# A new order and new engines for the pieces of a hand-ordered attention and mixture kernel

## The chip, the cores and the metric

The kernel runs on one core of a Trainium2 chip. The metric is the device time of one execution, in microseconds, from three timed runs; a profile of one execution goes with them. The engines of the core are named as in the profile: PE (TensorE), DVE (VectorE), ACT (ScalarE), POOL (GpSimd) and SP (SyncE, which issues all transfers here).

## What is computed

Three stages follow each other; the second takes the first's output as 1152 tokens of 512 features, the third the second's.

```python
# 1: attention, q k v of [2, 8, 576, 64]; four neighbours are averaged for a dense part, 7 neighbours seen by a local one
out_d = sm_attn(q_d, k_d, v_d)                       # on means of four
out_up = np.repeat(out_d, 4, axis=2)
mask = np.abs(pos[:, None] - pos[None, :]) < 4
x = out_up + softmax(where(mask, scale * q @ k.T, -1e9)) @ v
# 2: a rational activation; x [1152, 512], w_in [512, 2048], w_out [2048, 512] (float64)
h = x @ w_in
P = a[0] + a[1] * h + a[2] * h**2 + a[3] * h**3
Q = 1.0 + abs(b[0]) * abs(h) + abs(b[1]) * h**2
x = (P / (Q + 1e-06)) @ w_out
# 3: 8 experts, each token to the best one; w1 [8, 512, 1024], w2 [8, 1024, 512]; at most `capacity` tokens each
e = argmax(x @ w_gate); out = gate * (relu(x @ w1[e]) @ w2[e]), or 0 for a token that is dropped
```

## The kernel before

All work is cut into some 1,380 **pieces**, each a Python closure with a key. `plan_unit` makes those of the attention: a unit `u0` to `u7` is one batch and two heads, with loads (`lq`, `lk`, `lv`), transposes, local scores and their exponentials (`s`, `m`, `e`, `z`), the norm of the local softmax (`n0`, `n1`), the dense part (`ds` to `dp`; `dn` is its norm), the means of four queries, keys and values (`mq`, `mk`, `mv`) and the combination (`co`). `plan_w_in` and `plan_w_out` turn the float64 bits of one block of weights into float32 (`c1`, `c2`, `c3`, on DVE) and split each block into a high and a low part (`h` a cast, `o` a subtraction), since a product is made of three products of parts. `plan_moe1` is one chunk of 288 tokens (`m0` to `m3`) and a pair of the 16 row blocks of `w_in` (`_0` to `_7`): two groups of matmuls (`h0`, `h1`), then the rational function on a [128, 576] tile: `a` is |h|, `u`, `v1` and `v2` the cubic, `q1` and `q2` the denominator, `r1` and `r2` its reciprocal by a logarithm and an exponential, `f1` and `f2` a Newton step, `f3` the product. The first chunk also goes through `w_out` (`gh`, `go` split the result, `y` are the products) and one expert (`w1_`, `w2_`, `f1_`, `f2_`); the other chunks only need the gate's logits (`l`) and the routing (`rt`). A last count (`bd`) decides a branch that isn't taken here.

One table, `ORDER`, sets the order in which all pieces are emitted, and so the order of each engine's queue: every engine runs its instructions in that order, and waits at the first whose inputs are not there. A key may carry an engine (`m1_0_q1:G`): A, V or G for ACT, DVE or POOL. Buffers (44 of the common kind `G`, 5 for loads, 4 single and 2 double PSUM banks) go to the next taker in the order of release, so the table also sets who waits for whose buffer.

```python
def emit(self):                                   # class Plan
    for key, *_ in self.order:
        fn, needs, take, give = self.work[key]
        for t in take:
            self.held[t, key] = self.free[t].pop(0)
        if fn:
            fn()
        for x in give: ...
def q1():                                         # in plan_moe1
    if plan.engine.get(n + "q1") == "A":
        A.activation(out=d["r"], in_=d["z"], func=ACTF.Identity, scale=b1, bias=b0)
    else:
        vg(n + "q1").tensor_scalar(out=d["r"], in0=d["z"], scalar1=b1, scalar2=b0, ...)
```

`vg(key)` is DVE where the table says V, else POOL. The lines of the profile that matter: 383, 388 and 392 are the three conversions `c1`, `c2`, `c3`; 411 the low part of a `w_in` block, 893 that of a `w_out` or expert block; 473 and 476 to 478 the means of queries and keys, 494 and 495 those of values on POOL; 534 and 559 the norms; 726 and 728 `q1` on ACT and POOL; 731 `q2`; 734 and 737 `v1` and `v2`; 746, 749 and 753 `f1`, `f2` and `f3`. `v1` and `v2` read one of their inputs from PSUM; `f1`, `f2`, `f3` and the conversions read SBUF alone.

Of the kernel before, what the change touches and what calls it, by code (L numbers as in the profile page):

```python
# [22 lines left out]
ORDER = """
cz1 ci cm1:V cm2 ck2 warm22 warm9 u1_lq warm38 ck3 ck4 warm37 warm17 warm13 warm42 ck1 warm44 u1_tq u1_lk u1_tk cj:A u0_lq u0_lk u1_lw1
u1_cq:A wi0l u1_lwe u0_tq u1_ck:A cm3 u1_s0 u1_lw0 u1_lv cz0 u1_mq:G u1_mk:V u0_cq:A u0_mq:G u1_m0 wi7l u0_lw1 u1_ds u1_dm u0_tk u0_ck:V
u1_e0 u1_s1 u1_m1 u0_lv u2_lq warm8 u0_s1 u1_z0 u1_de u0_mk:G wi0c1 u1_e1 u0_s0 u1_dz u0_m1 u1_n0:G u1_lt0 wi0c2 u0_e1 u1_z1 u1_dn:G u0_m0
u1_lc0:V u0_ds u1_lt1 wi0c3 u1_lc1:V u0_e0 u1_n1:G u0_lwe u1_lt2 u0_dm u1_mv:G u1_dt0 u0_z0 u0_z1 u2_lk u1_dt1 u1_lc2:A u1_dc0:A u1_dc1:V
u1_lp2 u1_lp1 u0_mv:G u0_n0:V u0_n1:V u0_de wi0h:A u1_dp u1_dx:A u0_dz wi7c1 u1_lp0 u1_co0 u1_co2 u1_co1 u1_j2 u1_j1 u0_lt0 wi7c2 u2_tq
u2_tk wi2l u0_dn:G u0_dt0 u0_lt2 u0_lw0 u0_lc0:A wi0o:G u2_cq:A wi7c3 u2_ck:A wi1l u0_dt1 u3_lq u0_lc2:A u0_dc0:A wi2c1 wi2c2 u0_dc1:A
x0_1h:A u2_s1 u2_mq:G zs u0_lt1 u0_lc1:A u2_s0 u2_m1 u3_lk u0_dp u0_lp0 wi2c3 u2_e1 wi1c1 u2_m0 u0_dx:A wi1c2 u0_lp2 u0_lp1 u2_mk:G u0_co0  # L30
u2_z1 wi7h:V u0_co2 u2_e0 u2_ds u0_j1 cab wi3l u3_tq u2_n1:G u2_z0 u2_n0:G u2_dm u0_co1 wi2h:A u3_tk u2_lt2 u2_lt0 wi1c3 u3_cq:A u3_ck:A
u3_s1 x0_1o:G u2_lc2:V u3_mk:V u2_de u3_m1 u2_lc0:A u2_lt1 cb u3_s0 ccap u2_dz u2_lv wi2o:V u3_mq:G u3_m0 u2_dn:G wi3c1 u3_ds u2_lc1:A
u3_lwe u2_lwe u2_mv:G u2_lw1 u2_lw0 u3_dm u2_dt0 u3_e1 u4_lq u3_lv u4_lk u2_dt1 u2_dc1:V wi3c2 wi5l u3_e0 u3_z1 u2_lp2 wi3c3 ccf u3_z0
u3_n1:G u2_dc0:A u3_de u3_dz u3_lw0 u3_lw1 u3_mv:G u2_dp u2_dx:A u2_lp0 u2_co0 wi3h:A wi1h:A u2_lp1 u3_dn:V u3_lt2 u2_j0 u1_j0 u2_j1 u0_j2
wi7o:G u4_tq u4_tk u3_lc2:A u3_n0:V u2_co1 u2_co2 x0_0h:V u5_lq wi4l u4_cq:A u4_ck:A u4_mk:G u4_mq:G x0_0o:G u3_dt0 u3_lt0 u3_dt1 u3_dc0:V
u3_lt1 u3_lc1:A u3_dc1:A u4_s0 wi1o:V wi3o:V wi5c1 u3_dp u3_lc0:A x0_2h:A u3_lp0 u4_m0 wi5c2 u3_lp1 u3_dx:A u3_co0 wi5c3 u3_co1 u4_e0
u4_s1 x0_3h:A u3_lp2 x0_3o:G u4_m1 u4_ds x0_2o:V u3_co2 wi4c1 u4_z0 u4_dm wi5h:A u3_j1 u2_j2 u5_tq m0_0_h0 u4_e1 wi5o:G u4_n0:G u5_cq:A
wi4c2 u5_lk u4_de cna u5_tk wi4c3 u5_ck:A wi4h:A u4_lt0 wi14l wi6l wi14c1 u4_lt1 u4_dz u4_z1 wi14c2 u4_lc1:A m0_0_h1 u5_s0 u4_lc0:A m0_0_a
m0_0_u:A wi12l wi10l u5_s1 u5_lw0 u5_mq:G u5_lwe u4_lv u0_st wi6c1 u4_dn:G u4_dt0 wi14c3 wi6c2 u5_mk:G m0_0_q1:A wi11l u0_j3 u3_j0 u0_j0
u3_st u4_dc0:A u5_m0 wi12c1 wi6c3 wi6h:A u5_e0 wi10c1 u3_j2 u3_j3 m0_0_v1 u5_m1 u4_n1:G wi4o:G m0_0_q2:G u4_lw0 u4_lwe wi10c2 m0_0_v2  # L40
u4_lw1 m0_0_j u5_z0 wi12c2 wi10c3 wi8l u5_lv u5_e1 u5_ds u4_dt1 u4_mv:G u5_n0:G wi6o:G u4_dc1:A m0_1_h0 m0_1_h1 u5_z1 u5_dm m0_1_a
m0_1_u:A m0_2_h0 u4_lt2 m0_2_h1 wi9l wi12c3 u4_dp m0_0_r1 wi10h:A u5_de m0_1_v1 m0_2_u:A wi11c1 u4_dx:A m0_1_v2 u5_dz m0_1_j u4_lp0 u4_lp1
u5_n1:G wi14h:A u4_lc2:A m0_0_r2 m0_1_q1:G wi11c2 m0_2_v1 u5_lt2 wi11c3 u4_co0 m0_3_h0 m0_0_f1 u5_dn:G m0_1_q2:G u5_lw1 u4_co1 u6_lq
m0_2_a u5_lc2:A wi11h:A u5_lt0 u4_lp2 m0_2_q1:A u5_dt0 u5_dt1 u5_dc1:A m0_1_r1 wi9c1 u5_lc0:A m0_2_v2 m0_0_f2 m0_3_h1 u6_lk u4_j1 m0_2_j
u5_mv:G u6_tq u5_lt1 m0_2_q2:G wi11o:G wi8c1 u5_dc0:A u5_dp wi9c2 m0_3_u:A u6_cq:A wi8c2 u5_lc1:A u5_dx:A wi9c3 u6_mq:G u4_co2 m0_3_v1
wi9h:A u5_lp0 u5_co0 wi13l cwg u6_tk u7_lq wi8c3 u6_ck:A u5_lp1 u5_lp2 u5_co2 wi12h:A m0_3_a wi8h:A m0_1_r2 m0_2_r1 u6_s1 u6_mk:G u7_lk
m0_0_f3 u6_s0 wo1l u1_st u6_lw0 u6_j0 m0_3_v2 m0_3_j u1_j3 wi15l u5_j1 u7_tq u7_cq:A wi8o:G u6_ds wi9o:G u6_lv u6_m1 u6_m0 wi13c1 wi10o:G
u7_tk u7_lw1 zs8 m0_4_h0 m0_4_h1 u6_e1 m0_0_gh:A m0_1_f1 u6_dm u2_st wo2l zs2 wo1c1 m0_1_f2 u6_z1 u7_ck:A wi13c2 u5_co1 u6_e0 u7_s1 u7_s0
# [319 lines left out]

# [886 lines left out]
```

## Time and profile before

| | |
|---|---|
| time, median of 3 runs | 340.23 us (338.97 to 341.45) |
| profiled execution, span from first to last instruction | 340.3 us |
| DVE busy | 311.7 us, 92% |
| PE busy | 278.6 us, 82% |
| POOL busy | 238.3 us, 70% |
| ACT busy | 195.5 us, 57% |
| TensorE clock granted, mean | 0.894 of full |

The profiled execution's span is the median of the timed runs to 0.1 us, so nothing that could be told apart lies around it. Busy time is from the recorded start to the recorded end of each instruction, with overlaps counted once: an engine that has begun an instruction and is kept from running it counts as busy. An instruction of DVE starts some 0.07 us before the one ahead of it has ended, so durations add up to more than the time that passes.

### The profile page before, as it was taken

To read this page: it belongs to the slowest core of one execution; us is meant where nothing else is said; L and a number is where in the kernel's file an instruction comes from. 1 tells how busy PE (TensorE), PEld (TensorE's weight loads), DVE (VectorE), ACT (ScalarE), POOL (GpSimd) and SP (SyncE) were. 2 spreads that over 40 slices of the span, in tenths; PEclk is the share of its full clock that TensorE was granted. 3 is DMA by queue.
4 is the path that set the end of the run, shared out by engine and by line. 5 is a ranking of instruction groups with operands and counts; after the bars stand their busy time and mean duration, and the time that the engine had idled before them with its cause. 6 is when DMAs were issued, how large, how long until landed. Compare 5 with 4: busy or idle time off the path is not lost.

```text
span 340.3 us, 6602 instructions
## 1 busy us (share of the span) xinstructions
PE 278.6 (82%) x2366; PEld 250.9 (74%) x2366; DVE 311.7 (92%) x475; ACT 195.5 (57%) x488; POOL 238.3 (70%) x222
## 2 busy tenths in 40 slices
...
GB/s 161 231 183 193 160 242 107 229 208 156 137 268 223 189 279 256 64 218 65 123 71 1 0 37 35 3 49 230 2 0 2 154 3 62 3 0 0 2 21 57
DMA packets 50022, 37.62 MB, mean 111 GB/s; under 512 B 31680, under 2 KB 43712, under 8 KB 49984
## 3 DMA queue, kind: packets, MB, share of 16 engines
...
q8 instruction: 20, 0.33, 0.4%
q14 instruction: 18, 0.15, 0.2%
HBM read 32.42 MB, written 4.72 MB: 109 GB/s over the span
## 4 chain that ended last, share of the span: by engine, by line
DVE 65%; PE 17%; issue 8%; POOL 5%; ACT 3%; DVEq 0%; POOLq 0%; ACTq 0%
DVE rz L746 7%; PE ph L706 6%; DVE rz L749 6%; DVE ru L753 5%; DVE w L388 5%; DVE w2k L392 4%; DVE ru L734 4%; DVE ru L737 4%; DVE w2k L388 3%; DVE w L392 3%; DVE w L383 3%; PE psy L1054 3%; DVE w2k L383 3%; POOL rz L731 2%; DVE su L529 2%
## 5 line engine op out<-in xcount | busy, mean ns | idle before, releaser
L706 PE MATMUL ph<-xsp,whi 128*128 128x288 f32 x512 | 116.3, 323 | 19.6 <-DVE ru L737 17.9
L706 PEld LDWEIGHTS ph<-xsp,whi 128*128 128x128 f32 x512 | 90.6, 209 | 25.4 <-issue 12.2
L706 PE MATMUL ph<-xsp,wlo 128*128 128x288 f32 x256 | 80.4, 314 | 0.0
L731 POOL TENSOR_TENSOR rz<-rr,rz 128x576 f32<-128x576 f32 x31 | 52.5, 1701 | 6.9 <-ACT rr L726 6.2
L706 PEld LDWEIGHTS ph<-xsp,wlo 128*128 128x128 f32 x256 | 53.7, 210 | 0.0
L728 POOL TENSOR_SCALAR rr<-rz,absb 128x576 f32<-128x576 f32 x18 | 26.4, 1467 | 20.6 <-ACT rz L714 10.1
L714 ACT ACTIVATE rz<-ph 128x576 f32<-128x576 f32 x32 | 20.8, 650 | 31.7 <-PE ph L706 18.5
L746 DVE SCALAR_TENSOR_TENSOR rz<-rz,rr 128x576 f32<-128x576 f32 x32 | 35.3, 1104 | 3.6 <-POOL rz L731 2.1
L753 DVE SCALAR_TENSOR_TENSOR ru<-ru,na,rz 128x576 f32<-128x576 f32 x32 | 33.5, 1057 | 0.2
L749 DVE SCALAR_TENSOR_TENSOR rz<-rz,rr 128x576 f32<-128x576 f32 x32 | 32.6, 1029 | 0.2
L740 ACT ACTIVATE rr<-rz 128x576 f32<-128x576 f32 x32 | 21.8, 681 | 18.6 <-POOL rz L731 17.7
L719 ACT ACTIVATE ru<-ph,na 128x576 f32<-128x576 f32 x29 | 24.1, 831 | 6.5 <-PE ph L706 6.4
L893 POOL TENSOR_TENSOR lo<-w2k,hi 128x512 fp32r<-128x512 f32 x13 | 21.0, 1632 | 8.6 <-ACT hi L270 5.7
L524 ACT ACTIVATE sm<-pss,mn 128x70 f32<-128x70 f32 x72 | 22.0, 328 | 7.6 <-DVE mn L517 7.6
L737 DVE SCALAR_TENSOR_TENSOR ru<-ru,na,ph 128x576 f32<-128x576 f32 x32 | 25.8, 805 | 0.3
L968 PE MATMUL psy<-ghi,hi 128*128 128x288 f32 x64 | 22.0, 343 | 3.3 <-DVE x L607 3.3
L734 DVE TENSOR_TENSOR ru<-ru,ph 128x576 f32<-128x576 f32 x32 | 23.7, 742 | 0.2 <-ACT ru L719 0.2
L968 PE MATMUL psy<-glo,hi 128*128 128x288 f32 x64 | 21.3, 333 | 2.9 <-DVE glo L761 2.5
L968 PE MATMUL psy<-ghi,lo 128*128 128x288 f32 x64 | 21.2, 332 | 2.7 <-DVE lo L893 2.7
L743 ACT ACTIVATE rr<-rr 128x576 f32<-128x576 f32 x32 | 21.1, 679 | 0.3
L392 DVE SCALAR_TENSOR_TENSOR w2k<-w64o,w2k 128x512 uint32<-128x512 uint32 x16 | 18.4, 1160 | 0.0
L411 POOL TENSOR_TENSOR wlo<-w,whi 128x512 fp32r<-128x512 f32 x12 | 17.9, 1502 | 0.0
...
## 6 DMA issues: line engine op xcount, KB each, us to landing
...
```

Of the source, the lines that this page charges most:

```text
L388: V.scalar_tensor_tensor(out=t, in0=words()[1], scalar=0xC0000000, in1=t, op0=ALU.bitwise_and, op1=ALU.bitwise_or)
L392: V.scalar_tensor_tensor(out=t, in0=words()[0], scalar=29, in1=t, op0=ALU.logical_shift_right, op1=ALU.bitwise_or)
L706: PE.matmul(out=d["h"][:, i, 0:CH], lhsT=l[:, kk, :], rhs=r, start=(s == 0), stop=(s == 3 * KD - 1))
L719: A.activation(out=d["u"], in_=hv(), func=ACTF.Identity, scale=a3, bias=a2)
L728: vg(n + "q1").tensor_scalar(out=d["r"], in0=d["z"], scalar1=b1, scalar2=b0, op0=ALU.mult, op1=ALU.add)
L731: vg(n + "q2").tensor_tensor(out=d["z"], in0=d["r"], in1=d["z"], op=ALU.mult)
L734: V.tensor_tensor(out=d["u"], in0=d["u"], in1=hv(), op=ALU.mult)
L737: V.scalar_tensor_tensor(out=d["u"], in0=d["u"], scalar=a1, in1=hv(), op0=ALU.add, op1=ALU.mult)
L746: V.scalar_tensor_tensor(out=d["z"], in0=d["z"], scalar=QC, in1=d["r"], op0=ALU.add, op1=ALU.mult)
L749: V.scalar_tensor_tensor(out=d["z"], in0=d["z"], scalar=-2.0, in1=d["r"], op0=ALU.add, op1=ALU.mult)
L753: V.scalar_tensor_tensor(out=d["u"], in0=d["u"], scalar=a0, in1=d["z"], op0=ALU.add, op1=ALU.mult)
L968: PE.matmul(out=psy[m][:, 0:CH], lhsT=l, rhs=r, start=(kk == 0 and j == 0), stop=(kk == KF - 1 and j == 2))
```

## The change

Only the table changes (and comments go, by which every line number grows by one). All 1,379 entries are there before and after; hardly one keeps its neighbours. Of the diff, the second line of each table, as a sample:

```diff
-u1_cq:A wi0l u1_lwe u0_tq u1_ck:A cm3 u1_s0 u1_lw0 u1_lv cz0 u1_mq:G u1_mk:V u0_cq:A u0_mq:G u1_m0 wi7l u0_lw1 u1_ds u1_dm u0_tk u0_ck:V
+u1_e0 u0_lk u0_tq u1_mk:V u1_m1 u1_z0 u1_e1 u0_lv wi0c3 u1_ds u0_cq:A warm37 u0_tk u1_dm u1_n0:G wi2l u1_lw1 u1_lt0 u1_lwe u0_ck:A u0_s0
```

Of the 401 entries with an engine, POOL had 156 and has 72, ACT had 197 and has 235, DVE had 48 and has 94. Cut at the first product of the second chunk (`m1_0_h0`) and of the third (`m2_0_h0`), POOL's entries go from 69, 44 and 43 to 40, 9 and 23; DVE's from 22, 13 and 13 to 45, 27 and 22; ACT's from 101, 50 and 46 to 106, 66 and 63. By kind:

| pieces | from POOL to DVE (net) | from POOL to ACT (net) |
|---|---|---|
| `q1` | | 17 (and 1 from DVE) |
| `q2` | 11 | |
| low parts of weights (`wi` 4, `wo` 11, `w1` and `w2` 6) | 21 | |
| low parts of results (`go` 2, `y` 2) and of `x` (1) | 5 | |
| means: `mv` 6, `mk` 5, `mq` 3 | 14 | |
| norms: `n` 6, `dn` 3 | 9 | |
| high parts (casts) | | 8, net of one that comes to POOL |

From DVE to ACT go a net 2 `u`, 6 copies out of PSUM, 6 casts and one `q1`; DVE gets one scaling of the output (`f2c`).

Three places in the engines' queues. First POOL, where the second chunk's products begin and `w_out` is being split: before (`glo` is `go`, `lo` the low part of a weight, `rz` is `q2`, `rr` is `q1`, `xsp` a low part of x),

```order
L668 TENSOR_TENSOR xsp<-xr,xsp 128x288 x2
L761 TENSOR_TENSOR glo<-ru,ghi 128x576
L893 TENSOR_TENSOR lo<-w2k,hi 128x512 x3
L731 TENSOR_TENSOR rz<-rr,rz 128x576 x2
L728 TENSOR_SCALAR rr<-rz,absb 128x576
```

and after:

```order
L732 TENSOR_TENSOR rz<-rr,rz 128x576
L669 TENSOR_TENSOR xsp<-xr,xsp 128x288
L762 TENSOR_TENSOR glo<-ru,ghi 128x576 x2
L894 TENSOR_TENSOR lo<-w2k,hi 128x512
L732 TENSOR_TENSOR rz<-rr,rz 128x576 x2
L348 MEMSET iota 96x1
```

The low parts of `w_out` stand 13 times in POOL's queue before and twice after, and the scaling `rr` is gone from this stretch. Second DVE at the same place, before,

```order
L392 SCALAR_TENSOR_TENSOR w2k<-w64o,w2k 128x512
L734 TENSOR_TENSOR ru<-ru,ph 128x576
L746 SCALAR_TENSOR_TENSOR rz<-rz,rr 128x576
L737 SCALAR_TENSOR_TENSOR ru<-ru,na,ph 128x576
L749 SCALAR_TENSOR_TENSOR rz<-rz,rr 128x576
L383 TENSOR_SCALAR w2k<-w64o 128x512 x2
```

and after:

```order
L389 SCALAR_TENSOR_TENSOR w2k<-w64o,w2k 128x512
L762 TENSOR_TENSOR glo<-ru,ghi 128x576
L732 TENSOR_TENSOR rz<-rr,rz 128x576
L894 TENSOR_TENSOR lo<-w2k,hi 128x512
L750 SCALAR_TENSOR_TENSOR rz<-rz,rr 128x576
L384 TENSOR_SCALAR w2k<-w64o 128x512
```

`go`, `q2` and the low part of a weight now stand in DVE's own queue, between the conversions and the Newton steps. Third DVE at the start of the attention, before (`kd` and `qdb` are means of keys and queries, `mn` the minimum of local scores, `dm` that of dense ones),

```order
L473 TENSOR_REDUCE kd<-kt 128x144
L517 TENSOR_REDUCE mn<-pss 128x5
L544 TENSOR_REDUCE dm<-psd 96x3
L545 TENSOR_SCALAR dm<-dm 96x3
L466 TENSOR_SCALAR kt<-pskt 128x576
```

and after:

```order
L474 TENSOR_REDUCE qdb_144<-qt 64x3x48 x2
L518 TENSOR_REDUCE mn<-pss 128x5
L384 TENSOR_SCALAR w_216<-w_172 128x512
L389 SCALAR_TENSOR_TENSOR w_216<-w_172,w_216 128x512
L474 TENSOR_REDUCE kd<-kt 128x144
```

The mean of the queries is now DVE's work too, and the first conversion of weights stands ahead of the dense part.

## Rows read from the trace of the kernel before

**Rows 1.** The page's first part: span, busy time and instructions of each engine.

```profile
span 340.3 us, 6602 instructions
PE 278.6 (82%) x2366; PEld 250.9 (74%) x2366; DVE 311.7 (92%) x475; ACT 195.5 (57%) x488; POOL 238.3 (70%) x222
```

**Rows 2.** Stretches: length, busy PE, PEld, DVE, ACT, POOL (instructions); clock, DMA, GB/s.

```profile
0.00:132.00 132.00, 107.44 (x1146) 94.70 (x1147) 119.38 (x213) 88.21 (x306) 105.66 (x134) 0.86 0.81 199
132.00:228.00 96.00, 73.90 (x498) 65.73 (x496) 95.66 (x109) 49.38 (x87) 70.16 (x46) 0.91 0.22 66
228.00:329.00 101.00, 92.12 (x675) 86.18 (x676) 93.58 (x138) 55.94 (x94) 62.46 (x43) 0.94 0.13 42
329.00:340.30 11.30, 5.16 (x51) 4.25 (x51) 3.03 (x18) 1.94 (x3) 0.00 (x0) 0.83 0.20 59
```

**Rows 3.** Groups of DVE by form: count | busy us, mean ns | idle before.

```profile
L746 DVE SCALAR_TENSOR_TENSOR rz<-rz,rr 128x576 f32<-128x576 f32 x32 | 35.3, 1104 | 3.6 <-POOL rz L731 2.1 <-ACT rr L743 1.5
L753 DVE SCALAR_TENSOR_TENSOR ru<-ru,na,rz 128x576 f32<-128x576 f32 x32 | 33.5, 1057 | 0.2
L749 DVE SCALAR_TENSOR_TENSOR rz<-rz,rr 128x576 f32<-128x576 f32 x32 | 32.6, 1029 | 0.2
L737 DVE SCALAR_TENSOR_TENSOR ru<-ru,na,ph 128x576 f32<-128x576 f32 x32 | 25.8, 805 | 0.3
...
L392 DVE SCALAR_TENSOR_TENSOR w2k<-w64o,w2k 128x512 uint32<-128x512 uint32 x16 | 18.4, 1160 | 0.0
L388 DVE SCALAR_TENSOR_TENSOR w<-w,w 128x512 uint32<-128x512 uint32 x16 | 17.8, 1117 | 0.0
L392 DVE SCALAR_TENSOR_TENSOR w<-w,w 128x512 uint32<-128x512 uint32 x16 | 15.4, 961 | 0.0
L388 DVE SCALAR_TENSOR_TENSOR w2k<-w64o,w2k 128x512 uint32<-128x512 uint32 x16 | 15.0, 944 | 0.0
L383 DVE TENSOR_SCALAR w<-w 128x512 uint32<-128x512 uint32 x16 | 13.4, 837 | 0.0
...
L473 DVE TENSOR_REDUCE kd<-kt 128x144 f32<-128x576 f32 x2 | 1.5, 748 | 3.2 <-ACT kt L464 3.2
```

**Rows 4.** Timeline of DVE, three stretches: start us, duration us, instruction.

```profile
164.62 0.68 DVE L388 SCALAR_TENSOR_TENSOR w2k<-w64o,w2k 128x512 uint32<-128x512 uint32 x1
...
173.56 0.41 DVE L383 TENSOR_SCALAR w2k<-w64o 128x512 uint32<-128x512 uint32 x1
...
325.22 0.75 DVE L746 SCALAR_TENSOR_TENSOR rz<-rz,rr 128x576 f32<-128x576 f32 x1
325.89 0.81 DVE L737 SCALAR_TENSOR_TENSOR ru<-ru,na,ph 128x576 f32<-128x576 f32 x1
326.62 0.81 DVE L753 SCALAR_TENSOR_TENSOR ru<-ru,na,rz 128x576 f32<-128x576 f32 x1
```

**Rows 5.** Timeline of POOL and DVE about 222.6 us: start us, duration us, instruction.

```profile
222.63 1.43 POOL L731 TENSOR_TENSOR rz<-rr,rz 128x576 f32<-128x576 f32 x1
222.71 1.97 DVE L746 SCALAR_TENSOR_TENSOR rz<-rz,rr 128x576 f32<-128x576 f32 x1
```

**Rows 6.** Groups of POOL by form.

```profile
L731 POOL TENSOR_TENSOR rz<-rr,rz 128x576 f32<-128x576 f32 x31 | 52.5, 1701 | 6.9 <-ACT rr L726 6.2
L728 POOL TENSOR_SCALAR rr<-rz,absb 128x576 f32<-128x576 f32 x18 | 26.4, 1467 | 20.6 <-ACT rz L714 10.1 <-DVE rz L749 9.0 <-ACT rr L740 1.5
L893 POOL TENSOR_TENSOR lo<-w2k,hi 128x512 fp32r<-128x512 f32 x13 | 21.0, 1632 | 8.6 <-ACT hi L270 5.7 <-DMA xr<-xs 1.4 <-DVE rz L749 0.8
L494 POOL TENSOR_TENSOR vn<-vn 72x512 f32<-72x512 f32 x8 | 12.6, 1580 | 2.3 <-DMA vn<-in_v_dram 1.6 <-issue 0.4 <-DMA kn<-in_k_dram 0.3
...
L495 POOL TENSOR_TENSOR vd<-vn 72x256 f32<-72x256 f32 x8 | 8.6, 1076 | 0.6
...
L534 POOL TENSOR_TENSOR sm<-sm,su 128x280 f32<-128x280 f32 x7 | 5.6, 805 | 4.2 <-DVE su L530 3.9 <-DMA kn<-in_k_dram 0.4
```

**Rows 7.** The group of ACT that does `q1`, by form.

```profile
L726 ACT ACTIVATE rr<-rz,absb 128x576 f32<-128x576 f32 x13 | 11.2, 864 | 0.2
```

More of the change, by code (lines that the diff above doesn't have):

```diff
@@ L28 @@
[L28 to L31, printed above, removed]
@@ new lines @@
+u3_dc0:A u2_co1 u4_tq u3_lt0 u4_cq:A u3_dt1 u3_dc1:A u4_tk u4_ck:A cb wi4l u3_lt1 u3_dp wi3o:V u4_mq:G wi10l u3_lt2 wi1o:V u3_lc0:A
+u3_dx:A u3_lc1:A wi5c3 u3_lc2:A u3_lp0 u4_s1 x0_2h:A u5_lq wi4c1 u3_lp1 u4_mk:V u3_co0 u4_m1 u3_lp2 u4_e1 u4_ds wi10c1 u3_j1 wi5h:A wi4c2
+wi10c2 u5_tq u2_j2 u3_co1 u4_s0 u0_j0 u4_dm x0_3h:A u5_lk wi4c3 u5_cq:A wi6l u4_z1 x0_2o:G u4_m0 u5_mq:V x0_3o:G u5_tk u4_n1:V u5_lw1
+wi4h:A wi6c1 u4_lv u4_e0 u4_z0 m0_0_h0 wi5o:G u5_ck:A u4_n0:G u5_s0 wi6c2 u1_j0 u5_mk:V warm22 u3_co2 u5_s1 u5_m0 u5_m1 u4_de wi14l
@@ new lines @@
+m0_0_h1 u5_e1 u4_dz wi10c3 wi14c1 m0_1_h0 u1_st m0_0_u:A wi9l wi6c3 m0_0_a wi4o:G u4_lt0 u4_lt2 m0_0_q1:A wi14c2 u4_lw1 m0_0_v1 wi8l
+u4_mv:V u4_lw0 m0_0_v2 u5_lwe wi14c3 u4_dn:G m0_0_j u4_j0 m0_0_q2:G wi9c1 m0_1_h1 wi8c1 wi12l u5_z1 u5_e0 u0_st u5_ds m0_1_u:A wi6h:A
+m0_1_v1 wi6o:G m0_0_r1 wi10h:A u5_lv u5_dm m0_1_v2 u5_z0 u4_lc0:A wi8c2 m0_1_a m0_2_h0 u5_de u4_lt1 wi12c1 u0_j3 u5_lw0 wi14h:A u4_dt0
+u5_n0:V u4_lc2:A m0_1_j m0_1_q1:A m0_2_h1 m0_2_u:A u4_lc1:A m0_3_h0 wi12c2 m0_2_a wi9c2 m0_3_h1 u4_dt1 u5_n1:G m0_2_q1:A u4_dc1:A wi8c3
```

133 lines of the change are left out of this document (65 added, 68 removed).

## The prediction

> **What bounds the kernel now.** I read busy time first [rows 1]: DVE is busy for 311.7 of 340.3 us, no other engine above 82%. By stretches [rows 2], cut where the second and third chunks' products begin and where DVE's last `f3` ends, DVE idles 12.6 us of the first 132 (most of it the start), 0.3 of the next 96, 7.4 of the next 101 and 8.3 of the last 11.3. So DVE's queue is the kernel's length, up to a start and a tail of routing.
>
> But much of that busy time is no work. The reader should set a group's mean [rows 3] beside the same instruction on its own [rows 4]: `f1` takes 0.75 us after POOL's last instruction and 1.10 on average; `f3` 0.81 and 1.06; a conversion of line 388 0.68 and up to 1.12, one of line 383 0.41 and 0.84. `v2`, which reads PSUM, has 0.81 and 0.805: nothing is lost there. What keeps the others shows in [rows 5]: POOL's `q2` starts at 222.63 and ends at 224.06; DVE's `f1` starts 0.08 later and takes 1.97, ending 0.62 after POOL's. Of the 64 `f1` and `f2`, 24 take over 0.9 us, and every one of these ends 0.60 to 0.62 us after some POOL instruction has. **A DVE instruction on SBUF alone waits for the POOL instruction that runs, as long as that lasts.** I call this time held.
>
> Its size: in the groups shown, mean less undisturbed times count, 11.3 us for line 746, 8.9 for 749 (0.75 undisturbed, as 746), 7.9 for 753, 23.4 for lines 388 and 392 (four groups of 16; 0.68 for both), 6.8 for line 383 and 7.0 for its second group of 16 with the same mean: 65 us. The same count over DVE's other groups (sums, norms, subtractions on SBUF) adds some 21. So DVE holds about 226 us of own work and 86 held.
>
> **The change, part by part.** The sum is made against the profiled 340.3 us, which is the runs' median.
>
> *Work that DVE gains.* I count starts, not durations, 0.07 us less each, since DVE's instructions overlap by that [rows 4]. 11 `q2` have `f1`'s shape: 11 x 0.68 = 7.5. 21 low parts of weights have line 388's size: 21 x 0.61 = 12.8. 4 low parts of results: 2.7; one of x: 0.4. A mean of keys is in the rows, 0.75 [rows 3]: 5 x 0.68 = 3.4; one of queries is two reductions on half the partitions with as many elements each, 3 x 1.36 = 4.1. A mean of values on DVE stands nowhere; it reads 1,024 elements a partition where the keys' reads 576, so between 0.68 (nothing for the length) and 1.3 (all for it); I take 1.2, 7.2 in all, as the durations here go with elements. Norms of 280 to 432 elements by `f1`'s 576: 9 pieces, 4.0. Sum 42. It loses 2 `u`, 6 copies, 6 casts and one `q1`, of 0.35 to 0.8 us each, and gains one output scaling: some 6.5 off. **Net +35 us**, by place +22 in the first stretch, +2.5 in the second, +10.5 in the third. None of it is covered: it stands in the queue that bounds.
>
> *Work that POOL loses* [rows 6]: 17 `q1` x 1.47 = 25, 11 `q2` x 1.70 = 19, 21 low parts at about 1.6 (1.63 shown) = 33, 6 `mv` x 2.66 = 16; 30 others between 0.8 (line 534) and 2.2 us, mean 1.27: 38. Together 131 of its 238 us. Of POOL's undisturbed work the table leaves 56% in the first stretch, 21% in the second and 59% in the third: of 105.7, 70.2 and 62.5 busy us [rows 2] that is 59, 15 and 37.
>
> *What that gives back to DVE.* Split by stretch with undisturbed durations, DVE's own work was 84.7, 62.6 and 75.5 us (3.0 in the tail), so held were 34.7, 33.1 and 18.1 us: 0.33, 0.47 and 0.29 us for each busy us of POOL. I keep these rates for what POOL still does: 19.4, 6.9 and 10.7, that is 37 instead of 86. The bounds are 0 (each POOL instruction falls beside one of DVE's that reads PSUM) and 0.6 for each, 66 us, if DVE is hit nearly every time; I take the measured rates, since the mix of held and free kinds in DVE's queue hardly changes.
>
> *ACT* gains 18 `q1` x 0.86 [rows 7] and a dozen casts and copies, some 26 us on 195.5: 221 of some 326, two thirds busy. It isn't bound by that; if `a`, `r1` and `r2` now queue behind `q1`, the cost falls on `f1`, as a wait of DVE. In the trace before, all 32 `f1` waited 3.6 us for such inputs together [rows 3]; doubled or quadrupled that is 4 to 11 us, which I leave to the range, as the new order also places `f1` anew.
>
> *PE* does the same matmuls. In the second stretch it is busy 73.9 us [rows 2], in the third 92.1. There the sum can't go much under that: the granted clock was 0.91 and 0.94 of full, and I know no row that says it would be higher.
>
> *Loads and buffers.* SP issues the same transfers in another order. DMA was busy 81% in the first stretch and little after [rows 2]; a load that comes later delays the attention alone, and there DVE gets longer, not shorter, by the sum. I cost it at nothing; if it stalls DVE, it adds to the 12.6 idle us.
>
> *The tail* keeps its chain: the last `f3`, the last logits, a transpose, the routing of the last chunk, the count. 11.3 us as before; one output scaling of 0.7 us more on DVE is the risk there.
>
> The sum by stretches, own + held + idle: first 107.1 + 19.4 + 12.6 = 139.1 (7 more than before); second 65.1 + 6.9 = 72, but PE needs 74, so 74 (22 less); third 86.0 + 10.7 + 7.4 = 104.1 (3 more); tail 11.3. Together 328.5; the whole without stretches gives 226 + 35 + 37 + 28.6 idle = 326.6. **Forecast 327 us, 4% less.** The gain is nearly all in the second stretch, where POOL loses four fifths of its pieces.
>
> Here the Trainium skill, Perfetto Trace Analysis, section Optimizing Scalar/DVE Operations, speaks against the change: it advises to offload a saturated DVE to ScalarE or even GpSimd, and says that moving work between DVE and GpSimd might not help, as they share a read port. By that the 35 us would stand with little back for them. That is the second rival.
>
> **The rivals.**
>
> *Held time nearly vanishes.* With POOL at a third of the span instead of 70%, most of its instructions may fall where DVE reads PSUM or idles. Speaking for it: in the third stretch the rate was 0.29, in the second, with POOL at 73%, 0.47. Against: POOL starts when its inputs come, not when DVE is out of the way. First 119.7, second 74, third 93.4 (PE's 92.1 is just under it), tail 11.3: 298.
>
> *DVE pays for the added work and gets little back (slower).* Place: the attention, where 22 of the 35 us land and POOL keeps 59 us of work. Of the moved instructions there, norms and low parts work on SBUF alone, so they can themselves be held; a shorter POOL queue with more DVE instructions to hit need not hold less. If the 34.7 held us stay there, the first stretch is 154.4 and the whole 344; it is slower than before from 31 held us in that stretch on. In all stretches it would be 375, which the second forbids: 9 pieces can't hold 33 us. The rule quoted above is of this kind; the trace speaks against it so far as 86 of DVE's 312 busy us are held and end when POOL lets go.
>
> *The new order starves DVE.* It idled only some 13 us between start and tail, and every instruction waits in its queue's order. If DVE's 298 busy us have 40 idle ones instead of 28.6, from ACT's fuller queue, PE's products or a late load, the time is 338, no change. The measurement tells a per cent from no change; this is inside.
>
> **How the numbers follow.** The forecast 0.57, held time nearly gone 0.16, slower 0.14, starved 0.13. The forecast's own range is 312 to 336: held 22 to 46 us at the low and high rates (0.2 and 0.42), the mean of values at either bound (3 us less, 1 more). So faster by over 1% (under 336.9): the forecast nearly whole and the first rival, 0.72; within 1%: the starved case and a little of the forecast, 0.13; slower, 0.15. For 8 in 10, the range goes down nearly to the first rival's 298 and up nearly to the slower one's 344: **301 to 343**.
>
> **What would show it.** In the profile after: POOL at about 110 us or less; DVE at about 297, with `f1`, `f2` and `f3` near 0.8 to 0.95 us on average and `q2` on DVE near 0.75; the second stretch, from the second chunk's first product to the third's, at 72 to 78 us; the attention and first chunk at 135 to 142. Wrong would be a second stretch above 85, an `f1` still at 1.1 with POOL under 40% busy, or over 40 us of idle DVE. If the time is right but the first stretch is short, the rate there was mis-sized; if DVE isn't the fullest engine any more, the bound was mistaken.

## The result, and the profile after

The changed kernel takes 324.29 us (median of 4 runs, 321.76 to 325.87), the kernel before 340.84 in the same comparison (338.97 to 342.7): a ratio of 0.954, 95% interval 0.947 to 0.962. In a later comparison it had 324.51 and 0.954 (0.949 to 0.960). The profiled execution's span is 324.2 us. It is the slowest of the four runs: its time was 325.87 us, and in every run with both figures the time is 1.7 to 2.1 us more than the span. So the profiled execution of the kernel before, with a span of 340.3 us, took some 342 us by the same difference (an estimate), and was not one at the median of 340.23. Medians below are of all runs of a kernel, ratios of its fast runs alone, so that a ratio can differ a little from the quotient of the medians.

First the first lines of the page of the changed kernel (every line number is one higher than before):

```profile
span 324.2 us, 6535 instructions
PE 281.2 (87%) x2366; PEld 247.6 (76%) x2366; DVE 281.6 (87%) x524; ACT 217.6 (67%) x526; POOL 113.3 (35%) x121
```

Beside [rows 1], DVE has 49 more instructions and is busy 30 us less; POOL lost 125 of its 238 us. DVE and PE are now equally full. Next its stretches, with the columns of [rows 2], cut at the first product of each of the first three chunks and 0.2 us ahead of the end of DVE's last `f3` (313.1 us):

```profile
0.00:62.60 62.60, 51.54 (x533) 41.74 (x533) 46.98 (x110) 37.54 (x149) 22.12 (x40) 0.81 0.82 176
62.60:144.70 82.10, 66.78 (x613) 57.98 (x611) 74.25 (x139) 56.76 (x169) 41.98 (x34) 0.84 0.68 189
144.70:214.70 70.00, 67.13 (x502) 61.48 (x500) 66.14 (x115) 50.40 (x88) 15.82 (x26) 0.97 0.26 85
214.70:312.90 98.20, 91.26 (x687) 82.95 (x686) 90.18 (x141) 72.51 (x120) 33.37 (x23) 0.98 0.14 46
312.90:324.20 11.30, 4.45 (x43) 3.47 (x39) 4.02 (x23) 0.41 (x1) 0.00 (x0) 0.79 0.20 57
```

The first two rows together are the first stretch of [rows 2]: 144.7 us where it had 132. There the change loses 12.7 us. The second chunk takes 70.0 instead of 96, with POOL busy 16 us instead of 70: 26 us are gained, and not by PE's clock: DVE idled 0.3 us there before [rows 2], and in the run with the engines alone, below, the second chunk has a granted clock of 0.98 and still takes 83.2 us. PE is now as full as DVE in the chunks, 67.1 of 70.0 us and 91.3 of 98.2. The rest to the last `f3` takes 98.2 instead of 101, the tail 11.3 as before. DVE's idle time (length less busy) is 15.6 and 7.9 us in the first two rows, 3.9 in the second chunk.

Groups of DVE by form, the answer to [rows 3]:

```profile
L754 DVE SCALAR_TENSOR_TENSOR ru<-ru,na,rz 128x576 f32<-128x576 f32 x32 | 29.8, 940 | 0.0
L738 DVE SCALAR_TENSOR_TENSOR ru<-ru,na,ph 128x576 f32<-128x576 f32 x32 | 25.9, 809 | 3.3 <-ACT rz L715 2.8
L750 DVE SCALAR_TENSOR_TENSOR rz<-rz,rr 128x576 f32<-128x576 f32 x32 | 24.2, 770 | 0.0
L747 DVE SCALAR_TENSOR_TENSOR rz<-rz,rr 128x576 f32<-128x576 f32 x32 | 24.1, 758 | 2.6 <-ACT rr L744 2.6
...
L493 DVE TENSOR_REDUCE vd<-vn 72x256 f32<-72x1024 f32 x6 | 11.7, 1947 | 0.0
L393 DVE SCALAR_TENSOR_TENSOR w<-w,w 128x512 uint32<-128x512 uint32 x16 | 10.8, 677 | 0.0
L389 DVE SCALAR_TENSOR_TENSOR w2k<-w64o,w2k 128x512 uint32<-128x512 uint32 x16 | 10.7, 687 | 0.0
...
L894 DVE TENSOR_TENSOR lo<-w2k,hi 128x512 fp32r<-128x512 f32 x14 | 9.6, 706 | 0.0
L732 DVE TENSOR_TENSOR rz<-rr,rz 128x576 f32<-128x576 f32 x12 | 8.9, 751 | 0.0
L384 DVE TENSOR_SCALAR w2k<-w64o 128x512 uint32<-128x512 uint32 x16 | 8.0, 519 | 0.0
```

`f1` and `f2` fell from 1.10 and 1.03 us to 0.76 and 0.77, which is their time undisturbed [rows 4]; the conversions of lines 389 and 393 are at their 0.68 to 0.69. `v2`, which reads PSUM, has the 0.81 it always had. `f3` is still held a little (0.94 against 0.81), and so is line 384 (0.52 against the 0.41 of [rows 4]). And the group of POOL's `q2`, beside the first row of [rows 6]:

```profile
L732 POOL TENSOR_TENSOR rz<-rr,rz 128x576 f32<-128x576 f32 x20 | 40.8, 2044 | 92.0 <-ACT rr L727 77.2 <-issue 12.3 <-DVE rz L747 2.5
```

POOL's product takes 2.04 us on average now, where it had 1.70 in [rows 6] and 1.43 in [rows 5]. The mean hides two kinds: nine of the 20 take 1.46 us or less, and two take 4.33 and 5.64. The longest, with the last two DVE instructions that it meets (start, duration, and POOL's idle time ahead):

```profile
130.70 5.64 POOL L732 TENSOR_TENSOR rz<-rr,rz 128x576 f32<-128x576 f32 x1 [10.44 <-ACT rr L727]
...
134.38 0.68 DVE L389 SCALAR_TENSOR_TENSOR w2k<-w64o,w2k 128x512 uint32<-128x512 uint32 x1
134.99 0.74 DVE L735 TENSOR_TENSOR ru<-ru,ph 128x576 f32<-128x576 f32 x1
```

From 130.74 to 135.06 DVE runs seven instructions on SBUF alone without a pause, the last of them that of line 389; then comes `v1`, which reads PSUM, and POOL's product ends at 136.34, 1.28 us after line 389. So POOL too is kept waiting, through several instructions of DVE in a row. `f1` has no wait for POOL in the rows above, so this costs DVE nothing that shows. The Trainium skill, SBUF — State Buffer, section SBUF: two separate sides, describes the port pair that the two engines share as an exclusive lock: of a POOL instruction and a DVE instruction with two inputs in SBUF, the one that starts first has it for its whole instruction, and the other is blocked. The trace agrees that each blocks the other, with 1.97 us for an `f1` behind a `q2` that began 0.08 us earlier [rows 5], and with the 5.64 us here.

Last, what DVE waits for in the first stretch, first in the changed kernel and then in the kernel before (engine, line, releaser: us in total, times, longest; `x` is the sum of a unit's two parts):

```profile
DVE mn L518 <- PE pss L507: 6.6, 5, 2.7
DVE x L608 <- PE psx L601: 5.4, 5, 1.9
DVE dm L545 <- PE psd L541: 2.6, 3, 1.1
```

```profile
DVE mn L517 <- PE pss L506: 2.6, 3, 1.0
DVE x L607 <- PE psx L600: 0.7, 1, 0.7
DVE dm L544 <- PE psd L540: 0.4, 1, 0.4
```

These waits for PE's products grow from 3.7 to 14.6 us, by as much as DVE's idle time of the stretch does (12.6 to 23.5). In the attention DVE now waits for PE; what makes PE late there these rows don't show.

### The profile page after: what moved, and what is told of

Same layout as the page of the kernel before. It is cut to its first block, busy times and chain, and to the rows that moved or that the text cites. A ratio compares the mean times of both kernels' runs of the same rounds, so it can differ in the third digit from the quotient of the medians.

```text
span 324.2 us, 6535 instructions
## 1 busy us (share of the span) xinstructions
PE 281.2 (87%) x2366; PEld 247.6 (76%) x2366; DVE 281.6 (87%) x524; ACT 217.6 (67%) x526; POOL 113.3 (35%) x121
## 4 chain that ended last, share of the span: by engine, by line
DVE 48%; PE 29%; ACT 10%; issue 6%; DMA 3%; SPq 1%; POOL 1%; ACTq 0%; POOLq 0%; DVEq 0%
PE ph L707 7%; DVE ru L754 5%; DVE ru L738 5%; DVE ru L735 5%; DVE rz L747 4%; DVE rz L750 3%; PE psx L601 3%; PE pss L507 3%; DVE lo L894 3%; ACT rz L715 3%; PE pskt L457 2%; DVE w2k L389 2%; ACT ru L720 2%; DVE w L389 2%; DVE w2k L393 2%
## 5 line engine op out<-in xcount | busy, mean ns | idle before, releaser
L707 PE MATMUL ph<-xsp,whi 128*128 128x288 f32 x512 | 110.4, 310 | 12.0 <-DVE ru L738 8.6
L707 PEld LDWEIGHTS ph<-xsp,whi 128*128 128x128 f32 x512 | 84.9, 197 | 18.5 <-issue 8.8
L732 POOL TENSOR_TENSOR rz<-rr,rz 128x576 f32<-128x576 f32 x20 | 40.8, 2044 | 92.0 <-ACT rr L727 77.2
L707 PEld LDWEIGHTS ph<-xsp,wlo 128*128 128x128 f32 x256 | 50.1, 196 | 0.0
L754 DVE SCALAR_TENSOR_TENSOR ru<-ru,na,rz 128x576 f32<-128x576 f32 x32 | 29.8, 940 | 0.0
L727 ACT ACTIVATE rr<-rz,absb 128x576 f32<-128x576 f32 x31 | 26.6, 866 | 0.3
L747 DVE SCALAR_TENSOR_TENSOR rz<-rz,rr 128x576 f32<-128x576 f32 x32 | 24.1, 758 | 2.6 <-ACT rr L744 2.6
L750 DVE SCALAR_TENSOR_TENSOR rz<-rz,rr 128x576 f32<-128x576 f32 x32 | 24.2, 770 | 0.0
L507 PEld LDWEIGHTS pss<-kt,qt 64*64 64x64 f32 x288 | 12.8, 164 | 6.5 <-ACT kt L465 3.6
L507 PE MATMUL pss<-kt,qt 64*64 64x70 f32 x288 | 15.5, 262 | 2.0 <-ACT kt L465 2.0
L601 PE MATMUL psx<-pt,vm 70*64 70x64 f32 x224 | 14.5, 278 | 1.4 <-DVE x L608 1.0
```

The source lines that it names most:

```text
L507: PE.matmul(out=ps[p0:p0 + 64, (j - j0) * WIN:(j - j0 + 1) * WIN], lhsT=d["qt"][p0:p0 + 64, 64 * j:64 * j + 64], rhs=d["kt"][p0:p0 + 64, s ...
L707: PE.matmul(out=d["h"][:, i, 0:CH], lhsT=l[:, kk, :], rhs=r, start=(s == 0), stop=(s == 3 * KD - 1))
L732: vg(n + "q2").tensor_tensor(out=d["z"], in0=d["r"], in1=d["z"], op=ALU.mult)
L747: V.scalar_tensor_tensor(out=d["z"], in0=d["z"], scalar=QC, in1=d["r"], op0=ALU.add, op1=ALU.mult)
L750: V.scalar_tensor_tensor(out=d["z"], in0=d["z"], scalar=-2.0, in1=d["r"], op0=ALU.add, op1=ALU.mult)
L754: V.scalar_tensor_tensor(out=d["u"], in0=d["u"], scalar=a0, in1=d["z"], op0=ALU.add, op1=ALU.mult)
```

## The experiments

For all runs I split DVE's span into three. **Held** is, for each form of its instructions (line, operation and shapes), what their durations exceed that form's quickest tenth (the duration that a tenth of them stay under); by this count the kernel before has 86.8 us, as the prediction's count by groups gave. **Idle** is span less busy time. **Own** is the rest. The table has the profiled executions; times are medians, ratios are to the kernel before in the same comparison.

| run | order | engines | time | ratio | own | held | idle | POOL busy |
|---|---|---|---|---|---|---|---|---|
| before | old | old | 340.2 | | 225 | 87 | 29 | 238 |
| after | new | new | 324.3 | 0.954 (0.947-0.962) | 260 | 22 | 43 | 113 |
| engines alone | old | new | 335.7 | 0.986 (0.978-0.993) | 261 | 35 | 40 | 115 |
| order alone | new | old | 366.0 | 1.078 (1.069-1.087) | 224 | 68 | 71 | 224 |
| `q1` alone | old | 18 `q1` to ACT | 335.8 | 0.985 (0.973-0.997) | 226 | 79 | 28 | 213 |
| 53 pieces alone | old | 53 to DVE | 334.1 | 0.984 (0.975-0.994) | 251 | 55 | 27 | 167 |
| `mv` back | new | new, `mv` on POOL | 327.6 | 0.961 (0.955-0.968) | 251 | 29 | 46 | 125 |
| scratch products | new | new, POOL loaded | 358.8 | 1.056 (1.047-1.065) | 260 | 54 | 41 | 186 |
| warm-ups early | new | new | 322.4 | 0.949 (0.944-0.953) | 260 | 23 | 39 | 114 |
| seam at chunk 2, new engines | both | new | 325.7 | 0.955 (0.948-0.962) | 260 | 29 | 35 | 114 |
| seam at chunk 2 | both | both | 321.3 | 0.941 (0.935-0.948) | 237 | 53 | 31 | 155 |
| seam at pair 5 of chunk 1 | both | both | 318.1 | 0.937 (0.932-0.942) | 245 | 43 | 31 | 143 |
| seam at chunk 1 | both | both | 320.0 | 0.941 (0.937-0.946) | 253 | 27 | 37 | 131 |

### Order and engines apart

The table has two things in one: the sequence of keys, and the letter behind a key. The first kernel keeps the old sequence with the new letters, for instance

```diff
-m1_0_q1:G
+m1_0_q1:A
-u0_mv:G
+u0_mv:V
```

> The order of before with the engines of after. Held time (VectorE waiting while GpSimd runs) is the cause: GpSimd falls to about 110 us busy, VectorE's own work rises by 35 to 40 us and its held time falls from 86 to 20 to 40, so VectorE is busy 280 to 300 us and the time is 320 to 335 us, most or all of the gain. Rival, the new order is the cause: within 1% of 340 us, or slower by VectorE's added work.

The second keeps the letters and takes the new sequence, for instance ahead of the second chunk:

```diff
-wo1o:V u7_dx:A wg0c2:A wg0c3:A m1_0_h0 m1_0_h1 m1_0_a
+wo3h:A u7_co0 wo0o:G u7_co1 m1_0_h0 wo6l wg0c2:A u7_co2
```

> The order of after with the engines of before. Held time is the cause: GpSimd near 238 us busy again, VectorE's held time 80 to 90 us, so 338 us or more. Rival, the order is the cause: 322 to 332 us, with VectorE's held time near 86 us but less idle elsewhere.

Measured: 335.73 us (334.74 to 338.31) and 366.02 us (364.35 to 368.56). Engines alone give a third of the gain (1.4% of 4.6%), not the most or all that I expected; the order alone costs 26 us; together they give 16. The first lines of the two pages, old order with new engines and then new order with old engines:

```profile
span 336.5 us, 6550 instructions
PE 275.7 (82%) x2366; PEld 246.2 (73%) x2366; DVE 296.2 (88%) x524; ACT 217.6 (65%) x526; POOL 114.8 (34%) x121
```

```profile
span 362.6 us, 6580 instructions
PE 292.1 (81%) x2366; PEld 255.9 (71%) x2366; DVE 291.8 (80%) x475; ACT 194.6 (54%) x488; POOL 223.8 (62%) x222
```

In the second DVE is busy 20 us less than before and idle 71 us, 42 more. Its waits over its first 157 us say for what:

```profile
DVE mn L517 <- PE pss L506: 12.1, 9, 4.9
DVE dm L544 <- PE psd L540: 7.5, 4, 3.5
DVE x L607 <- PE psx L600: 4.5, 3, 3.1
```

The same three waits as in the changed kernel, longer. That POOL's 69 pieces of the attention stand in an order made for 40 may be why; no run tests it. Held time was 68 us here, not the 80 to 90 expected, though POOL is busy 224. For the engines alone the table is the prediction's own sum: own +36 us (I had said 35), held 35 (I had said 37). What I hadn't said is +12 us of idle. From there to both together held time falls by another 13 us, idle time grows by 2 and own work stays: with the new engines, the order's gain of 11 us is held time. It also moves DVE's own work ahead, from the second chunk (70 to 62 us) to the first stretch (105 to 110): part of what the one loses the other gains. The second chunk with the engines alone, in the columns of [rows 2]:

```profile
138.88:222.11 83.23, 69.64 (x497) 60.69 (x496) 77.09 (x125) 56.25 (x98) 17.36 (x13) 0.98 0.23 74
```

### Two parts of the engine change alone

Only the 18 `q1` go to ACT, all else is as before:

```diff
-m1_0_q1:G
+m1_0_q1:A
```

> Before, with only the 18 scalings q1 moved to ScalarE as after has them. VectorE gets no work, GpSimd loses some 25 us. Held time: at 0.36 us per busy us of GpSimd VectorE's held time falls by 9 us, so 329 to 334 us. Rival, only GpSimd's links in the chain counted, and those have slack: 340 us within 1%. Rival, ScalarE's queue then delays f1: slower than 344 us.

Only 53 pieces with two inputs (`q2`, low parts, norms) go from POOL to DVE:

```diff
-wo5o:G
+wo5o:V
-u1_n1:G
+u1_n1:V
```

> Before, with only the 53 two-input pieces moved from GpSimd to VectorE as after has them (low parts, q2, norms; no means, nothing to ScalarE). VectorE gains some 30 us of own work, GpSimd loses some 77 us. Held time: at 0.36 us per busy us 28 us of held time go, so about 342 us, an even exchange; at the lower rate that after shows (0.19) up to 38 us go, 332 us. Rival, VectorE pays for all that it is given: 365 us or more.

Measured: 335.84 us (333.08 to 338.2) and 334.13 us (333.18 to 337.85). The `q1` took 25 us from POOL and 8 of held time from DVE, at no cost that shows; the time was expected at 329 to 334. The 53 pieces cost DVE 26 us of own work and saved 32 us held, with idle time unchanged, so the time lies between the 332 and the 342 us expected: an engine that bounds the kernel was given 53 pieces more and the kernel became 1.6% faster. Here the advice of the Trainium skill that the prediction weighed (Perfetto Trace Analysis, Optimizing Scalar/DVE Operations: moving work between these two might not help) and the measurement differ, and the measurement decides: with POOL busy 70% of the time it helps, by a little.

### Is it the hold, or POOL as a link in the chain?

Held time could be read wrongly: with a shorter POOL queue every result of POOL also comes earlier. So the changed kernel got POOL work that nobody waits for:

```diff
+pad = res.tile([128, 576], F32, name="pad")
+plan.load = {f"m{c}_{mp}_{x}" for c in range(1, 4) for mp in range(8) for x in ("q2", "f2")}
+def dummy():
+    ...                                                         # a memset of pad, once
+    G.tensor_tensor(out=pad, in0=pad, in1=pad, op=ALU.mult)      # emitted behind each key in plan.load
```

> The changed kernel with 48 GpSimd products of one scratch tile [128, 576] with itself, two for each pair of row blocks in the second to fourth chunk, whose result nobody reads (69 us more of GpSimd by the 1.43 us of one undisturbed). If VectorE's instructions on SBUF wait while GpSimd runs, at 0.19 to 0.45 us for each busy us of GpSimd, VectorE's f1, f2 and f3 get longer than their 0.76 to 0.94 us, VectorE's held time grows by 13 to 31 us, and the time goes to 334 to 355. If GpSimd cost time only as a link in the chain from q1 to f1, the durations on VectorE stay as they are, its idle time grows a little where a q2 comes late, and the time is 324 to 330.

Measured: 358.8 us (356.78 to 362.14), 34 more than the changed kernel. The scratch products and DVE's three Newton pieces (`f3`, `f1`, `f2`) and `v2` in the groups by form:

```profile
L295 POOL TENSOR_TENSOR pad<-pad 128x576 f32<-128x576 f32 x48 | 68.8, 1434 | 1.7
```

```profile
L765 DVE SCALAR_TENSOR_TENSOR ru<-ru,na,rz 128x576 f32<-128x576 f32 x32 | 37.1, 1170 | 0.0
L758 DVE SCALAR_TENSOR_TENSOR rz<-rz,rr 128x576 f32<-128x576 f32 x32 | 34.9, 1094 | 1.1 <-ACT rr L755 1.0
L761 DVE SCALAR_TENSOR_TENSOR rz<-rz,rr 128x576 f32<-128x576 f32 x32 | 29.9, 946 | 0.0
L749 DVE SCALAR_TENSOR_TENSOR ru<-ru,na,ph 128x576 f32<-128x576 f32 x32 | 25.9, 809 | 3.5 <-ACT rz L726 3.1
```

`f1` is back at 1.09 us, `f3` at 1.17, `v2` stays at 0.81, and the wait of `f1` for its input shrank from 2.6 to 1.1 us. Held time grew by 32 us for 73 us more of busy POOL, 0.44 for one, and DVE's idle time not at all. One such pair in the timeline (start, duration):

```profile
257.84 1.67 POOL L295 TENSOR_TENSOR pad<-pad 128x576 f32<-128x576 f32 x1
258.42 1.70 DVE L758 SCALAR_TENSOR_TENSOR rz<-rz,rr 128x576 f32<-128x576 f32 x1
```

The scratch product ends at 259.51, the `f1` at 260.12, 0.61 us later, as the 24 of the kernel before did. There is no data between the two. So the hold is shown as a cause of its own, worth 30 us and more; the chain theory doesn't explain it. My range of 334 to 355 was just too low.

### What lengthens the attention

From the kernel before to the changed one the first stretch grew by 12.7 us. By the count above DVE's own work in it grew by 28.5 us (82 to 110), its held time fell by 27 (38 to 11) and its idle time grew by 10.9; 4.6 of the 12.7 us come before the first chunk's first product (58.0 and 62.6 us), 8.1 behind it. Three candidates. First DVE's own work: the means of values take 1.95 us on DVE, which I had taken at 1.2. They go back to POOL:

```diff
-u0_mv:V
+u0_mv:G
```

> The changed kernel with one thing undone: the six means of values are back on GpSimd, where VectorE took 1.95 us each for them. If VectorE's queue sets the length of the attention too, VectorE loses 11.7 us there and is held some 3 us more by GpSimd's 16 us: the second chunk's first product comes at 136 to 138 us instead of 144.7, and the time is about 316. If in the new order the attention hangs on the chain through TensorE and back (VectorE idles 23.5 us of it), the start of the second chunk stays at 143 to 146 and the time within 322 to 326.

Measured: 327.56 us (327.37 to 327.8), the second chunk's first product at 147.2 us. DVE lost 9 us of own work, got 7 of held time (I had said 3) and 4 of idle time for it, and nothing was gained: both figures lie just above the second theory's. The run doesn't clear DVE's queue, since that was nearly as full as before with held time; it shows that work taken off DVE isn't gained here when POOL gets it.

Second the clock. The change spread the eight warm-up products, which the old order has among its first keys; here they go back to the start:

```diff
-ci cm1:G ck1 cz1 cz0 u1_lq u1_tq
+ci cm1:G ck1 cz1 cz0 warm22 warm9 u1_lq warm38 warm37 warm17 warm13 warm42 warm44 u1_tq
```

> The changed kernel with eight of its warm-up products of the identity moved to where the order of before has them, ahead of the first transposes (the change spread them over the attention and the tail). If TensorE's granted clock over the first 60 us (0.65 and 0.75 between 20 and 60 us in the changed kernel's profile, 0.87 twice in the profile of the run with the scratch products, whose program is the same up to there and which begins the second chunk 4.8 us earlier) follows from a late first rise, the second chunk begins at 138 to 141 us and the time is 318 to 321. If it follows from the attention's own gaps, or if these products only delay the first transposes, the second chunk begins at 143 to 148 and the time is 323 to 328.

Measured: 322.44 us (320.66 to 324.47) beside 324.51 for the changed kernel in the same comparison, whose intervals overlap; the second chunk begins at 144.1 us, against 144.7 and 143.5 in the changed kernel's two profiles. The missing early warm-ups aren't the reason: the second chunk begins no sooner with them. With it the changed kernel ran once more:

> The changed kernel once more, beside the three others of this call. 322 to 326, a ratio of about 0.954. Its first stretch varies between executions, as the same program up to the second chunk has shown (139.9 and 144.7 us): if TensorE's clock makes that difference, a profile with a shorter first stretch has a higher granted clock between 20 and 60 us, and one with a longer stretch a lower.

Measured: 324.51 us (321.57 to 326.28). The windows from 20 to 60 us of three profiles of one and the same program up to there: the changed kernel, again the changed kernel, and the one with scratch products, which only come later:

```profile
20.00:40.00 20.00, 17.59 (x180) 14.52 (x179) 15.43 (x39) 11.95 (x51) 6.33 (x8) 0.65 0.80 159
40.00:60.00 20.00, 17.72 (x199) 13.86 (x198) 16.14 (x39) 13.23 (x49) 6.13 (x8) 0.75 0.79 183
```

```profile
20.00:40.00 20.00, 17.57 (x185) 14.53 (x184) 16.44 (x42) 12.52 (x52) 7.35 (x9) 0.70 0.79 161
40.00:60.00 20.00, 17.60 (x204) 13.80 (x202) 16.35 (x39) 13.71 (x54) 5.07 (x7) 0.79 0.82 192
```

```profile
20.00:40.00 20.00, 16.10 (x211) 12.62 (x211) 17.62 (x44) 14.20 (x57) 9.95 (x11) 0.87 0.98 193
40.00:60.00 20.00, 17.91 (x218) 15.07 (x216) 17.17 (x43) 13.77 (x55) 5.53 (x6) 0.87 0.76 178
```

With a granted clock of 0.65 and 0.75 the second chunk begins at 144.7, with 0.70 and 0.79 at 143.5, with 0.87 at 139.9. The clock and the attention's length go together, over 5 us; which is the cause and what made the clock differ from one execution to the next was not tried. But the clock doesn't set the two orders apart. The kernel before has, in the same windows:

```profile
20.00:40.00 20.00, 16.65 (x208) 14.25 (x210) 19.73 (x40) 14.47 (x63) 16.87 (x19) 0.85 0.87 187
40.00:60.00 20.00, 17.52 (x173) 15.50 (x174) 17.39 (x36) 11.07 (x43) 15.54 (x15) 0.57 0.77 169
```

Its mean of 0.71 is that of the changed kernel's first profile (0.70), and its second chunk begins at 132.0 instead of 144.7.

Third the order itself. Four kernels have the old order up to a seam and the new one behind it. The first of them has the new engines throughout, with the seam at the second chunk's first product:

```diff
 wo1o:V u7_dx:A wg0c2:A wg0c3:A
-m1_0_h0 m1_0_h1 m1_0_a m0_5_q1:A
+m0_3_q2:V zs1 m0_3_r1 m0_2_f3 zs3 m0_3_r2
```

(Ahead of the minus line stands the end of the old order; the plus line is the beginning of what the new order has ahead of `m1_0_h0` and the old one hasn't.)

> Engines of the changed kernel; the order of before up to the second chunk's first product, the new order for everything behind it. If what an order does is settled place by place, the attention is that of the run with the old order and the new engines (138.9 us) and what follows is that of the changed kernel (179.5 us): 318. If the chunks run faster only because the new order had already done more by then, the second chunk's first product still comes at 139, but the rest takes 185 to 198 us: 324 to 337.

Measured: 325.69 us (324.56 to 326.82), no better than the change. The second chunk began at 137.2, 7.5 us earlier; but its second pair came at 160.7, where the changed kernel has 160.1. The lead was gone there: the new order seems to count on work that the old one does later. The next has, besides, the old engines up to the seam, but for `q1`:

```diff
-u0_mv:V u1_n1:V wo2o:V
+u0_mv:G u1_n1:G wo2o:G
```

> As the run before it in this list (old order up to the second chunk's first product, new order behind), and up to that point also the engines of before, save that the scalings q1 are on ScalarE; behind it the engines of the change. If the places add up, 128.8 us as in the run with q1 alone, and 179.5 behind: 308. If GpSimd's fuller queue in the attention leaves arrears for the second chunk, or the attention of the run with q1 alone was short only for what it put off, 315 to 325.

Measured: 321.33 us (319.64 to 322.72): second chunk at 135.9, its second pair at 158.3. Most of the lead is gone again. A repeat of this kernel beside the changed one gave no result, so its 321.33 us and the changed kernel's 324.29 are of two comparisons. Next the seam was moved ahead, to the first chunk's fifth pair, where `w_out` isn't split yet:

```diff
 u6_m0 wi13c1 wi10o:G u7_tk u7_lw1 zs8
-m0_4_h0 m0_4_h1 u6_e1 m0_0_gh:A
+u4_j0 zs2 xr1_0 wi12o:G wi13c2 m0_3_q1:A
```

> As the run with the old order and the old engines up to the second chunk (and q1 on ScalarE), but the new order and engines take over earlier, at the fifth pair of the first chunk. If that run lost its attention's lead of some 7 us because the new order found work undone at the seam that it expects done, an earlier seam, still ahead of the splitting of w_out, leaves less undone: the fifth pair at 97 to 99 us as there, the second pair of the second chunk at 154 to 157 instead of 158, and the time is 316 to 319. If the arrears come from the attention and from the splitting of w_in itself, they only move, and the time is 320 to 325.

Measured: 318.1 us (316.96 to 321.21), 2% under the changed kernel's 324.51 in the same comparison; the ratios' intervals, 0.932 to 0.942 and 0.949 to 0.960, lie apart. The fifth pair came at 98.6 us, the second pair of the second chunk at 154.4: the lead is kept. This version is faster than both kernels. At last the seam at the first chunk's first product:

```diff
 wi5h:A u3_j1 u2_j2 u5_tq
-m0_0_h0 u4_e1 wi5o:G u4_n0:G
+cna wi10l u4_e1 wi10c1 wi4c2 wi10c2
```

> As the run with the seam at the first chunk's fifth pair, but the new order and engines take over at the first chunk's first product. If the new order costs time in the attention ahead of that product alone (it came at 55.1 us there, at 61.3 and 62.6 in the changed kernel), the lead of 6 us is kept to the end and the time is 316 to 319. If the new order is slower in the rest of the attention too, which runs beside the first chunk's first half, the lead shrinks: the fifth pair comes at 100 to 104 us instead of 98.6, and the time is 320 to 325.

Measured: 320.0 us (319.1 to 321.96), the median at the rival's lower end, but the marks are those of the first theory: fifth pair at 98.1 us, and a first stretch as short as there. Its profile, with a span of 317.4 us, is of the fastest of its six runs, so it says little about the median, and the ratios of the two versions (0.937 to 0.946 and 0.932 to 0.942) overlap: which seam is better isn't shown. First its stretches to the second chunk, then those of the version with the later seam:

```profile
0.00:55.80 55.80, 45.95 (x547) 39.59 (x547) 46.28 (x103) 36.66 (x153) 42.49 (x79) 0.88 0.94 196
55.80:138.50 82.70, 66.82 (x601) 58.51 (x601) 74.89 (x141) 55.24 (x159) 38.97 (x28) 0.83 0.67 188
```

```profile
0.00:55.10 55.10, 47.34 (x539) 40.46 (x540) 45.99 (x99) 35.38 (x147) 42.41 (x78) 0.81 0.92 188
55.10:139.00 83.90, 63.11 (x610) 55.94 (x608) 81.86 (x135) 55.97 (x166) 51.36 (x44) 0.88 0.67 190
```

Up to the first product the old order and engines take 55 to 56 us here, the new ones 61.3 and 62.6; from there to the second chunk these four profiles take 82 to 84, and what follows takes 179 to 180. So what the change loses to a mixture of both lies in its first 62 us. Not all of it is the order's: the kernel before itself has its first product at 58.0, and the run with scratch products, the changed program up to there, at 58.4. DVE's own work is greater there with the new order and engines (43 us, against 34 with the earliest seam), and so is its idle time (16 against 9). Which pieces of the new sequence make the gaps is left open. Against the kernel before the picture is another one: from the first product to the second chunk it takes 74.0 us, so that none of these mixtures is as quick there.

## Why the prediction came true

The forecast was 327 us, the time 324.3: in the range and 0.8% off. The sum was one of a span, 326.6 or 328.5 by stretches, beside 324.2. Such a hit owes much to luck, since two of its terms were wrong by 14 to 15 us each, with opposite signs. And one of the signs that the prediction gave for being wrong came: DVE idles more than 40 us. DVE is busy 281.6 us, not 297, which is no longer clearly above PE's 281.2.

**The bound and the hold.** DVE held up by POOL was the right reading of [rows 3 to 5]: taking POOL's work away brought `f1` and `f2` to their undisturbed times, and giving it work that nobody needs brought the hold back, at 0.44 us for each of POOL's, in the span of my rates of 0.29 to 0.47. The rule in bold says one half of it: DVE on SBUF waits for a POOL instruction that runs, but a POOL instruction that comes while DVE is busy on SBUF can be the one that waits, as the 5.64 us of one `q2` show. In the changed kernel 9 of the 20 `q2` on POOL have their 1.42 to 1.46 us, so they wait for nothing.

**Net +35 us on DVE.** Own work went from 225 to 260 us, more of it in the first stretch than I had it (110 us, where the sum has 107) and less in the other two (62 and 84, where it has 65 and 86). The means of values, estimated at 1.2 us, took 1.95, outside my bound of 1.3; low parts (0.71) and `q2` (0.75) were as said. The length of the row read was too small a measure for the means: 1,024 elements took 2.6 times as long as the keys' 576. POOL came to 113 us, a little over the 107 to 110, since its own `q2` went from 1.70 to 2.04.

**Held stays at its rates: 37 us.** This step failed for the whole change: 21.7, just under the 22 of the forecast's own range. It held for the engines alone, with 35. The rates of the old order are not those of the new one: in the first stretch 11 us where I had 19.4. The run with the old order had just those 19.4 there, and a first stretch of 138.9 where I had said 139.1. So the new order brings POOL's work to where DVE is hit less. In the traces, of POOL's instructions of over 0.3 us in the first stretch, 26 of 56 hold up a DVE instruction with the engines alone and 12 of 57 in the changed kernel; DVE idles beside 9% and 16% of POOL's time there, and behind that stretch it reads PSUM beside 32% and 46%. Both ways that I had named, idle moments and neighbours that read PSUM, are thus seen; how much each gives, no run shows.

**Idle assumed unchanged: 28.6 us.** This failed too: 42.6. Of the 14 us more, nearly all lie in the attention, 23.5 where I had 12.6 in that stretch, and 3.9 in the second chunk. I had left a longer wait to ACT's queue; what came was waiting for PE, 14.6 us in the attention instead of 3.7. Engines alone raise it by 12, with the order alone it is 71. I had named the case as a rival (a new order starves DVE, 40 us idle, 338 us), and its idle time came; with my 37 us held it would have made about 340. The 15 us of held time that fell beyond my 37 paid for it.

**By stretches.** The attention and first chunk were 144.7 (139.1, expected at 135 to 142), the second chunk 70.0 (74, expected at 72 to 78), the third stretch 98.2 (104.1), the tail 11.3 (11.3). For the second I took PE's 73.9 busy us as a floor. That floor gave way, a size that I had wrong: the same matmuls took 67.1 us of PE at a granted clock of 0.97 instead of 0.91, with 3 us of gaps where it had had 22.

**ACT** has 217.6 us (221), and `f1` waits 2.6 us for its inputs (3.6 before): its queue cost DVE nothing that shows. **The rivals:** held time went some two fifths of the way from my 37 us to the first rival's zero, and DVE paying without return is refuted by the 53 pieces alone.
